# Value rows moved to partitions 32 to 95, mean rows placed by GpSimd and ScalarE copies, gate columns made by halves of the bank

## The chip, the core and the metric

The kernel runs on one core of one Trainium2 chip. The metric is the device time of one execution in microseconds (us); a kernel's figure is the median of several executions, 483.07 us before the change.

## The reference, cut to what matters

Two stages follow each other: a windowed attention with block summaries, and an expert layer that picks 384 tokens for each expert in turn.

```python
B, H, S, D = 4, 8, 768, 64
k_sum = k.reshape(B, H, 24, 32, D).max(axis=3)      # one key per block of 32
v_sum = v.reshape(B, H, 24, 32, D).mean(axis=3)     # one value per block of 32
scores_l = where(|i - j| < 16, q @ k.T / 8, -1e9)
scores_s = q @ k_sum.T / 8 + log(32)
a = softmax(concat(scores_l, scores_s))
x = a @ concat(v, v_sum)                            # then laid out as 3072 tokens x 512
logits = x @ w_gate                                 # 8 experts
# (token, expert) pairs in falling order of logit, at most 384 tokens an expert, one expert a token
out[tokens of e] = relu(x[tokens of e] @ w1[e]) @ w2[e]
```

## The kernel before

**Tiles.** A batch has 12 query blocks of 64 tokens. Two blocks and all heads of one sort make a unit `u`; two units (even and odd heads) make a tile `t`, so there are 24 tiles, six for each of the 4 batches. For a query block the kernel holds 120 key columns: 64 + 2 x 16 tokens of the window (`W` = 96) and 24 block summaries (`C` = 120). The values stand in a tile `VW` (two buffers, for even and odd batches) of 120 partitions x 12 blocks x 8 heads x 73 columns: in one row the 64 value columns, 8 gate columns (value times gate weights) and a 1 for the sum of the softmax.

**Steps of a tile.** `s` (PE, L407) makes the scores; `m` (DVE, L415) adds the mask and takes the row maximum; `e` (ACT, L422) takes the exponential; `t` (PE, L138) transposes; `c` (ACT or DVE, L183/L185) copies the transpose to `pt`; `pv` (PE, L447) multiplies with `VW`; `n` (DVE, L467 to L472) divides; `xw` (POOL's queue, L499) writes the token rows `xd` to memory.

**Steps of a batch, before its tiles.** `k`, `q`, `vt`, `w` are loads issued by SyncE (SP). `w` (L348) brings the value rows of two query blocks each into partitions 0 to 63 of `VW`, six times a batch; L350 brings the last 32 rows into partitions 64 to 95. `vh` (POOL, L297) and `vs` (DVE, L303) sum the values of a block of 32. `vg` (PE, L312) multiplies the values with the gate weights; its results for the even blocks stand in rows 0 to 63 of the bank `VL` and for the odd blocks in rows 64 to 127. `vgc` (L185 or L183) copies them as gate columns into `VW`. `h` (POOL or ACT) copies the first 32 rows of the next block into partitions 64 to 95, the part of the window that reaches into it. `vm` (PE) transposes the mean rows, `vmc` (L328 or L330) copies them into partitions 96 to 119 of block 0, and `place` puts the same 24 rows beside the other 11 blocks: for batch 0 by eleven copies of ACT and POOL, for batches 1 to 3 by one DMA of SP (L340) from partitions 96 to 119 of block 0 to the same partitions of blocks 1 to 11.

**What sets the order.** Every step is a task with an engine, a cost, its predecessors and a rank. `plan` keeps a clock for each engine from these costs and writes the tasks out one by one, by start and rank; `TUNE` and `RANK` hold the numbers. So the order on each engine is fixed when the program is built, and an instruction that waits holds all that stands behind it on its engine. SP's loads share a ring in which each issue waits for the DMA eight places ahead of it.

**After attention** the routing of expert 0 and eight experts follow (PE lines L929, L940, L963, L908).

Of the kernel before, what the change touches and what calls it, by code (L numbers as in the profile page):

```python
# [19 lines left out]
B, H, S, D = 4, 8, 768, 64  # L20
# [3 lines left out]
NB = S // BLK  # L24
# [32 lines left out]
def attention_moe(ctx, tc, qT, kT, vT, v73, wg, w1r, w2r, cst, out, dbg=None, dbi=None):  # L57
# [131 lines left out]
    with ExitStack() as att:  # L189
# [64 lines left out]
        for b in range(B):  # L254
# [32 lines left out]
            for p in range(HP):  # L287
# [5 lines left out]
                @task(("vh", b, p), "pool", 0.9, [("vt", b, p)] + ([("vs", b, p - 1)] if p else []), u0 + TUNE["vs"] + 0.1 * p)  # L293
# [5 lines left out]
                @task(("vs", b, p), "dve", 0.5, [("vh", b, p)], u0 + TUNE["vs"] + 0.1 * p)  # L299
# [5 lines left out]
                @task(("vg", b, p), "pe", 0.9, [("vt", b, p)] + ([("vg", b, p - 1)] if p else [("m", u0 - 6 + k) for k in range(2)] + [("vmc", b - 1, 1)] + [("vgc", b - 1, int(b == 1), x) for x in range(2)] if b else ["constants"]), u0 + TUNE["vg"] + 0.1 * p)  # L305
# [46 lines left out]
            for j, (k0, k1) in enumerate(((0, 2), (2, NQ // 2)) if b == 0 else ((0, NQ // 2),)):  # L352
                for x in range(2):
                    @task(("vgc", b, j, x), {"act": 0.42 + 0.06 * (k1 - k0), "dve": 0.3 + 0.07 * (k1 - k0)}, None, [("vg", b, HP - 1)] + [("w", b, k) for k in range(k0, k1)], u0 + TUNE["vc"] + 0.1 * x + j)
                    def _(eng, b=b, x=x, k0=k0, k1=k1):
                        vw = VW[b % 2]
                        for s in range(2):
                            copy(eng, vw[:QB, 2 * k0 + x:2 * k1:2, s::2, s * D:s * D + E], VL[b][x * QB:x * QB + QB, k0:k1, s::2])
                        if x == 0 and k1 == NQ // 2:
                            copy(eng, gates(vw[QB:W, NQ - 1]), VL[b][QB - 2 * HALO:QB, k1].rearrange("p (k s) e -> p k s e", s=2))  # L360

                for k in range(k0, k1):
                    @task(("h", b, k), "pool" if b else {"pool": 1.2 if k else 0.65, "act": 1.0 if k else 0.55}, 1.2 if k else 0.65, [("vgc", b, j, x) for x in range(2)] + ([("vgc", b, 0, x) for x in range(2)]), u0 + TUNE["hv"] + 0.1 * k)
                    def _(eng=None, b=b, k=k):
                        i = max(2 * k - 1, 0)
                        copy(eng or nc.gpsimd, VW[b % 2][QB:W, i:2 * k + 1], VW[b % 2][:2 * HALO, i + 1:2 * k + 2])
# [23 lines left out]
        for u in range(U):  # L390
# [40 lines left out]
            def _(eng, u=u):  # L431
# [4 lines left out]
                  [("c", u), ("c", u | 1 if t < NT - 1 else u), ("w", b, i // 2)] + ([("place", b)] if b else [("place", b, i - s + x) for x in range(2) if i - s + x]) + [("h", b, k) for k in (i // 2, i // 2 + 1) if k < NQ // 2]  # L436
# [14 lines left out]
        for t in range(NT):  # L451
# [22 lines left out]
            if t + 1 in ends:  # L474
                @task(("lr", t), "dve", 0.53 if t < NT - 3 else 0.27, [("n", t)], u + TUNE["n"] + (2.5 if t < NT - 4 else 0.0))
# [21 lines left out]
            @task(("xw", t), "pool", 0.6, [("xm" if t == NT - 1 else "n", t)], u, 0.8)  # L497
# [543 lines left out]
```

## Time and profile before

| | us |
|---|---|
| median of 3 runs | 483.07 (481.05 to 485.16) |
| the profiled execution | 481.45 |
| its span, first to last instruction | 479.6 |
| last `pv` of attention starts | 149.54 |
| last write of token rows issued by POOL | 154.80 |

The span is the profiled execution without 1.85 us that lie around it. The first 155 us are attention, the rest is routing and experts. Engines are PE (matmul), PEld (its weight load), DVE, ACT, POOL and SP; "idle before, releaser" names what ended an engine's wait, and "issue" is a wait for nothing that the profile shows. Partitions are the 128 rows of the on-chip memory.

### The profile page before, as it was taken

The numbers are of one execution on the slowest core, as the hardware profiler recorded it, in microseconds if no ns is written. First come the engines' busy times: TensorE is split into PE (matmuls) and PEld (weight loads), VectorE is DVE, ScalarE is ACT, GpSimd is POOL, SyncE is SP. The second block draws the span as 40 slices with busy tenths as digits, with TensorE's granted clock in tenths as the row PEclk, the third lists the DMA queues.
The fourth block names the chain that finished last, engine by engine and source line by source line (L and its number), as shares of the span: only waits on it lengthen the run. The fifth ranks groups of instructions, "written<-read, shape, count | busy, mean of one in ns | idle before, by whom it ended". The sixth has DMA issues, their size and how long they took to land.

```text
span 479.6 us, 11577 instructions
## 1 busy us (share of the span) xinstructions
PE 433.3 (90%) x4381; PEld 377.4 (79%) x4381; DVE 341.4 (71%) x1285; ACT 219.6 (46%) x469; POOL 128.2 (27%) x190
## 2 busy tenths in 40 slices
PE   7667949959795489999999999999999999999995
PEld 7557739759684379878978978978988988988985
DVE  5367774956887688888879878978978877662520
ACT  5586664953794035426306414424424524652420
POOL 3375552642611120023023024004003203501001
PEclk9669886976898569999999999999999999999998
DMA  8999999997422064085067058039129118950101
GB/s 302 236 402 226 355 201 247 359 224 204 103 84 94 27 236 191 0 275 216 1 230 262 1 187 282 24 126 326 41 93 322 77 44 299 388 186 22 45 22 44
DMA packets 25555, 84.02 MB, mean 175 GB/s; under 512 B 3461, under 2 KB 3845, under 8 KB 25117
## 3 DMA queue, kind: packets, MB, share of 16 engines
q1 hardware_dynamic: 19740, 62.84, 42.3%
q0 software_dynamic: 5760, 20.45, 11.7%
q8 instruction: 34, 0.56, 0.5%
q14 instruction: 21, 0.16, 0.1%
HBM read 68.06 MB, written 13.37 MB: 170 GB/s over the span
## 4 chain that ended last, share of the span: by engine, by line
PE 81%; issue 6%; DMA 6%; DVE 5%; SPq 1%; ACT 0%; POOLq 0%; DVEq 0%; POOL 0%
PE h L940 28%; PE y L963 25%; PE o L447 6%; PE t L138 5%; PE l L312 3%; PE s L407 3%; DMA vw<-v 3%; PE r L533 2%; PE y L908 2%; PE h L138 2%; PE x L407 2%; DMA vt<-vT 2%; DMA xg<-xd,idx 1%; DVE xq L472 1%; PE h L929 1%
## 5 line engine op out<-in xcount | busy, mean ns | idle before, releaser
L735 POOL DMA_INDIRECT xg<-xd,idx x24 | 24.9, 1037 | 165.5 <-issue 119.3
L963 PE MATMUL y<-bh,hl 128*128 128x512 f32 x168 | 67.6, 402 | 0.0
L963 PE MATMUL y<-bl,hh 128*128 128x512 f32 x168 | 67.2, 400 | 0.0
L963 PE MATMUL y<-bh,hh 128*128 128x512 f32 x168 | 66.6, 397 | 0.0
L720 ACT ACTIVATE ah<-raw 128x1024 fp32r<-128x1024 f32 (+1 forms) x36 | 34.3, 970 | 65.2 <-DMA raw<-w1r 37.7
L945 ACT ACTIVATE hh<-h 128x384 fp32r<-128x384 f32 x64 | 31.5, 492 | 68.5 <-PE h L940 66.9
L422 ACT ACTIVATE pe<-sm,mx 128x120 f32<-128x120 f32 x192 | 58.2, 385 | 4.1 <-DVE mx L415 4.0
L940 PE MATMUL h<-xh,al 128*128 128x384 f32 x256 | 55.7, 339 | 0.0
L940 PE MATMUL h<-xl,ah 128*128 128x384 f32 x256 | 55.0, 339 | 0.0
L940 PE MATMUL h<-xh,ah 128*128 128x384 f32 x244 | 54.7, 342 | 0.0
L890 POOL DMA_INDIRECT out<-y,idx x24 | 29.2, 1216 | 86.2 <-ACT y L888 63.4
L948 DVE SCALAR_TENSOR_TENSOR hl<-h,hh 128x384 fp32r<-128x384 f32 x64 | 34.7, 549 | 24.4 <-ACT hh L945 23.9
L940 PEld LDWEIGHTS h<-xh,al 128*128 128x128 f32 x256 | 45.3, 188 | 0.0
L940 PEld LDWEIGHTS h<-xl,ah 128*128 128x128 f32 x256 | 45.1, 188 | 0.0
L940 PEld LDWEIGHTS h<-xh,ah 128*128 128x128 f32 x244 | 42.9, 188 | 0.6
L183 ACT ACTIVATE pt<-t 120x512 f32<-120x512 f32 x44 | 25.2, 591 | 36.7 <-PE t L138 36.5
L447 PE MATMUL o<-vw,pt 120*64 120x73 f32 x736 | 34.9, 253 | 7.1 <-issue 5.0
L447 PEld LDWEIGHTS o<-vw,pt 120*64 120x64 f32 x736 | 30.8, 156 | 11.2 <-issue 7.5
L723 DVE TENSOR_TENSOR bl<-raw,bh 128x1024 fp32r<-128x1024 f32 x32 | 38.9, 1217 | 0.8 <-ACT bh L720 0.8
L723 DVE TENSOR_TENSOR al<-raw,ah 128x1024 fp32r<-128x1024 f32 (+1 forms) x36 | 39.1, 1100 | 0.1
L963 PEld LDWEIGHTS y<-bh,hh 128*128 128x128 f32 x168 | 31.6, 188 | 5.6
L963 PEld LDWEIGHTS y<-bl,hh 128*128 128x128 f32 x168 | 31.6, 188 | 5.5
(183 smaller groups left out, 809.2 us busy)
## 6 DMA issues: line engine op xcount, KB each, us to landing
raw<-w1r SPq DMA_DIRECT2D x32, 512.0 KB, 5.5
raw<-w2r SPq DMA_DIRECT2D x32, 512.0 KB, 4.5
vw<-v SPq DMA_DIRECT2D x24, 292.0 KB, 19.0
xd<-xq POOLq DMA_DIRECT2D x24, 288.0 KB, 6.8
kd<-kT SPq DMA_DIRECT2D x16, 400.0 KB, 9.7
vt<-vT SPq DMA_DIRECT2D x16, 400.0 KB, 8.6
qt<-qT SPq DMA_DIRECT2D x3, 1536.0 KB
vw<-vw SPq DMA_DIRECT2D x3, 602.2 KB
```

What stands on the lines that cost most here:

```text
L138: nc.tensor.transpose(o, i, idn)
L183: nc.scalar.activation(o, i, AF.Copy)
L422: nc.scalar.activation(PE_[u][:, p], SM[u][0][:, p], AF.Exp, bias=SM[u][1][:, p:p + 1], scale=-1.0)
L447: nc.tensor.matmul(po(t, s)[x * 64:x * 64 + 64, p], PT[u][:, p, x * 64:x * 64 + 64], VW[b % 2][:C, i - s + x, 2 * p + s], start=True, stop ...
L720: nc.scalar.activation(hi[:, c], raw[:, c], AF.Copy)
L723: nc.vector.tensor_tensor(lo[:, c], raw[:, c], hi[:, c].bitcast(F32), op=OP.subtract)
L735: nc.gpsimd.indirect_dma_start(out=x, out_offset=None, in_=xd, in_offset=bass.IndirectOffsetOnAxis(ap=idx[:, c:c + 1], axis=0))
L890: st = nc.gpsimd.indirect_dma_start(out=out, out_offset=bass.IndirectOffsetOnAxis(ap=ROUND[r][1][:, c:c + 1], axis=0), in_=y, in_offset=None)
L940: nc.tensor.matmul(ph, a[:, d], b[:, d], start=k == d == 0, stop=k == 2 and d == 3, skip_group_check=r == 0 and f in early)
L945: nc.scalar.activation(hh[:, f], ph, AF.Relu)
L948: nc.vector.scalar_tensor_tensor(hl[:, f], ph, 0.0, hh[:, f].bitcast(F32), op0=OP.max, op1=OP.subtract)
L963: nc.tensor.matmul(py[c], a[:, f, s], b, start=f == 0 and i == 0, stop=f == 7 and i == 2)
```

## The change

The value rows of a block now stand in the order halo, block, means: rows 0 to 31 of `VW` are the first 32 tokens of the window, rows 32 to 95 the other 64. The six loads of a batch go into partitions 32 to 95; one load brings rows 0 to 31 of block 0; `h` copies partitions 64 to 95 of a block into partitions 0 to 31 of the next. In the bank `VL` the first six blocks have rows 0 to 63, the last six rows 64 to 127, and `vgc` has four copies (first or last six blocks, lower or upper 32 rows), each waiting for three of the six loads. The DMA of `place` is gone; all four batches have eleven `place` copies on POOL or ACT. A `pv` of a tile needs the `place` copies of its own two blocks and one `h`. All numbers of `RANK` and five of `TUNE` are replaced, so every engine's order is another.

```diff
-    sm=4, spe=0, sdve=0.11, sact=0, spool=1.08, m=0.569, e=2.793, t=2.307, c=0.793,
+    sm=4, spe=0.03, sdve=0.14, sact=0.59, spool=1.01, m=0.569, e=2.793, t=2.307, c=0.793,
...
                     for i in range(NQ + 1):
-                        c, x = min(i * QB, SP - QB), i % 2 * QB
-                        o = VL[b][x:x + QB, i // 2, 2 * p:2 * p + 2].rearrange("p h e -> p (h e)")
+                        k, x = (i // 2, i % 2) if i < NQ else (NQ // 2, 0)
+                        c = QB * (NQ // 2 * x + k) + 2 * HALO if i < NQ else 0
+                        o = VL[b][x * QB:x * QB + QB, k, 2 * p:2 * p + 2].rearrange("p h e -> p (h e)")
...
-            for i in range(1, NQ) if b == 0 else ():
-                @task(("place", b, i), {"pool": 0.63, "act": 0.6}, None, [("vmc", b, 0), ("vmc", b, 1)], TUNE["p0"] + 0.5 * i)
-                def _(eng, i=i):
-                    copy(eng, VW[0][W:C, i], VW[0][W:C, 0])
-
-            @task(("place", b), "sp", 0.6, [("vmc", b, 0), ("vmc", b, 1)] + ([("pv", u0 - NQ - 1)] if b > 1 else []), u0 + TUNE["pl"], 1.7) if b else lambda f: None
-            def _(b=b):
-                vw = VW[b % 2]
-                nc.sync.dma_start(vw[W:C, 1:].rearrange("p n h d -> p n (h d)"), vw[W:C, :1].rearrange("p n h d -> p n (h d)").to_broadcast([NB, NQ - 1, H * VD]))
+            for i in range(1, NQ):
+                @task(("place", b, i), {"pool": 0.67, "act": 0.67}, None, [("vmc", b, 0), ("vmc", b, 1)] + ([("pv", u0 - 2 * NQ + i // 2 * 2 + 1)] if b > 1 else []), u0 + TUNE["pl"] + 0.5 * i)
+                def _(eng, b=b, i=i):
+                    copy(eng, VW[b % 2][W:C, i], VW[b % 2][W:C, 0])
...
-                    nc.sync.dma_start(vw[:QB, 2 * k:2 * k + 2], bass.AP(tensor=v.tensor, offset=v.offset + 2 * k * QB * H * VD, ap=[[H * VD, QB], [QB * H * VD, 2], [1, H * VD]]))
-                    if k == NQ // 2 - 1:
-                        nc.sync.dma_start(vw[QB:W, NQ - 1], v[S:])
+                    if k == 0:
+                        nc.sync.dma_start(vw[:2 * HALO, 0], v[:2 * HALO])
+                    nc.sync.dma_start(vw[2 * HALO:W, 2 * k:2 * k + 2], bass.AP(tensor=v.tensor, offset=v.offset + (2 * k * QB + 2 * HALO) * H * VD, ap=[[H * VD, QB], [QB * H * VD, 2], [1, H * VD]]))
...
+            for x in range(2):
+                for y in range(2):
+                    @task(("vgc", b, x, y), {"act": 0.55 + (0.22 if x == y == 0 else 0.0), "dve": 0.55 + (0.22 if x == y == 0 else 0.0)}, None, [("vg", b, HP - 1)] + [("w", b, k) for k in range(3 * x, 3 * x + 3)], u0 + TUNE["vc"] + x + 0.1 * y)
...
+                        copy(eng, dst, VL[b][x * QB + 32 * y:x * QB + 32 * y + 32, :6].rearrange("p n (k s) e -> p (n k) s e", s=2))
...
+                    i = max(2 * k, 1)
+                    copy(eng or nc.gpsimd, VW[b % 2][:2 * HALO, i:2 * k + 2], VW[b % 2][QB:W, i - 1:2 * k + 1])
```

On SP, from the loads of batch 1's mean rows on, this stands before (`vw_102` is the value tile of batches 1 and 3, `vw_101` of batches 0 and 2; `24x11x584` is `place`):

```order
L291 DMA vt<-vT 128x800 x3
L340 DMA vw_102<-vw_102 24x11x584
L260 DMA qt_99<-qT 128x3072
L348 DMA vw_101<-v 64x2x584 x6
L350 DMA vw_101<-v 32x584
```

and this now:

```order
L291 DMA vt<-vT 128x800 x3
L260 DMA qt_99<-qT 128x3072
L345 DMA vw_101<-v 32x584
L346 DMA vw_101<-v 64x2x584 x6
L291 DMA vt<-vT 128x800 x4
```

The DMA that waited for DVE's copy of the mean rows is gone from between the loads, and the queries and values of batch 2 follow batch 2's `vt` directly.

On POOL, around the tiles of batch 1, before (`32x584` and `32x1168` are `h`, `vh` the block sums of batch 2, `kd` the window and summary columns of batch 2's keys):

```order
L185 COPY vw_102<-vw_102 32x584
L185 COPY vw_102<-vw_102 32x1168 x5
L185 COPY kd<-kd 128x12x36
L185 COPY kd<-ks 128x12x24
L185 COPY kd<-kd 128x12x36 x2
L297 TENSOR_TENSOR vh<-vt 128x384
```

and now:

```order
L297 TENSOR_TENSOR vh<-vt 128x384
L185 COPY vw_102<-vw_102 24x584 x3
L297 TENSOR_TENSOR vh<-vt 128x384
L497 DMA xd<-xq_103 128x576
L185 COPY vw_102<-vw_102 24x584
L185 COPY kd<-kd 128x12x36
L185 COPY kd<-ks 128x12x24
L185 COPY vw_102<-vw_102 24x584
L185 COPY kd<-kd 128x12x36
```

Ten copies of `24x584` for batch 1 are new on POOL, and they stand between the `vh` and `kd` work of batch 2 and the writes of token rows.

On DVE, at the start of batch 0, before:

```order
L303 TENSOR_REDUCE vs<-vh 128x24
L185 COPY pt<-t 120x512
L185 COPY vw_101<-l 64x4x4x8 x2
L303 TENSOR_REDUCE vs<-vh 128x24
L273 TENSOR_REDUCE ks<-kd 128x24 x2
```

and now:

```order
L185 COPY pt<-t 120x512 x2
L303 TENSOR_REDUCE vs<-vh 128x24
L185 COPY vw_101<-l 32x24x2x8 x3
L331 TENSOR_SCALAR vw_101<-x 24x4x2x64
```

The last `vs` of batch 0 stood behind the gate copies that wait for the value loads and now stands ahead of them; the copy of the mean rows follows on the same engine.

## Rows read from the trace of the kernel before

**Rows 1.** Stages of attention: length, busy us of each engine, granted clock, DMA.
```profile
core 0: us, PE busy (x) PEld busy (x) DVE busy (x) ACT busy (x) POOL busy (x), PEclk, DMA share, GB/s
12.00:58.00 46.00, 35.83 (x658) 30.56 (x654) 28.25 (x138) 30.77 (x84) 23.85 (x37) 0.78 1.03 304
58.00:73.00 15.00, 8.17 (x188) 7.27 (x188) 10.41 (x72) 8.99 (x28) 8.84 (x13) 0.82 1.03 217
...
94.00:105.00 11.00, 6.00 (x133) 5.01 (x132) 7.92 (x53) 7.86 (x24) 7.50 (x12) 0.85 1.03 196
...
sum 143.00, PE 113.10 PEld 97.17 DVE 99.41 ACT 92.27 POOL 64.37; mean PE 16.16 PEld 13.88 DVE 14.20 ACT 13.18 POOL 9.20
```
**Rows 2.** DMA view: GB/s in 40 slices of 1 us, 0 to 40 us.
```profile
GB/s 0 48 285 384 346 211 346 385 374 412 422 406 400 290 173 206 203 208 206 206 213 223 216 296 368 399 406 407 386 391 404 402 406 408 399 454 436 366 198 175
```
**Rows 3.** The same, 120 to 160 us.
```profile
GB/s 0 135 128 128 139 105 5 0 0 251 309 60 272 9 0 16 0 221 74 0 101 210 0 124 179 0 0 281 14 76 221 290 18 0 0 46 249 0 8 0
```
**Rows 4.** The page's DMA issues: count, KB each, us to landing; and the instruction queue.
```profile
q8 instruction: 34, 0.56, 0.5%
...
vw<-v SPq DMA_DIRECT2D x24, 292.0 KB, 19.0
xd<-xq POOLq DMA_DIRECT2D x24, 288.0 KB, 6.8
...
vw<-vw SPq DMA_DIRECT2D x3, 602.2 KB
```
**Rows 5.** Timeline, start of batch 0: start, duration, work, idle before and releaser.
```profile
25.48 0.69 ACT L183 ACTIVATE vw<-l 64x128 f32<-64x128 f32 x3 [2.91 <-DMA vw<-v]
26.20 0.50 DVE L185 COPY vw<-l 64x128 f32<-64x128 f32 x2 [4.42 <-ACT vw L183]
26.62 0.54 DVE L303 TENSOR_REDUCE vs<-vh 128x24 f32<-128x384 f32 x1
...
29.06 0.59 ACT L328 ACTIVATE vw<-x 24x512 f32<-24x512 f32 x1
```
**Rows 6.** Chain of waits: start, length, what.
```profile
12.19 13.27 DMA vw<-v
...
31.81 1.97 PE o L447 x32
...
43.11 2.48 issue
...
125.58 2.50 issue
```
**Rows 7.** Timeline of PE around the first tiles of batches 1 and 2.
```profile
58.26 1.24 PE L447 MATMUL o<-vw,pt 120*64 120x73 f32 x32
...
71.82 1.36 PE L312 MATMUL l<-wgp,vt 128*64 128x16 f32 x22 [5.44 <-issue]
...
73.09 2.10 PE L447 MATMUL o<-vw,pt 120*64 120x73 f32 x30
...
78.55 2.21 PE L447 MATMUL o<-vw,pt 120*64 120x73 f32 x32
...
94.30 1.24 PE L447 MATMUL o<-vw,pt 120*64 120x73 f32 x32
...
104.65 0.83 PE L312 MATMUL l<-wgp,vt 128*64 128x16 f32 x13 [4.69 <-issue]
105.32 2.19 PE L447 MATMUL o<-vw,pt 120*64 120x73 f32 x32
```
**Rows 8.** Stages after the two stops: length, PE busy, granted clock, DMA.
```profile
76.00:82.00 6.00, 6.00 (x84) 0.57 1.03 252
82.00:94.00 12.00, 11.60 (x231) 1.00 1.02 387
...
105.00:118.00 13.00, 13.00 (x210) 0.60 0.89 252
```
**Rows 9.** Waits: who for whom, us in total, times, longest.
```profile
SPq L340 <- DVE dn L468: 17.1, 2, 11.0
```
**Rows 10.** Timeline: the `place` copies of batch 0 on ACT and POOL.
```profile
29.98 3.58 ACT L183 ACTIVATE vw<-vw 24x584 f32<-24x584 f32 x6
...
30.02 3.15 POOL L185 COPY vw<-vw 24x584 f32<-24x584 f32 x5 [0.25 <-ACT vw L328]
```
**Rows 11.** Groups by line, 0 to 175 us: busy us, mean ns.
```profile
L183 ACT ACTIVATE vw<-l 64x192 f32<-64x192 f32 (+3 forms) x18 | 4.2, 276 | 7.1 <-PE l L312 4.0 <-DMA vw<-v 2.9
...
L185 DVE COPY vw<-l 64x192 f32<-64x192 f32 (+1 forms) x6 | 1.8, 334 | 5.5 <-ACT vw L183 5.5
```
**Rows 12.** Waits of POOL, 24 to 130 us.
```profile
POOL vh L297 <- DVE vs L303: 25.9, 9, 7.4
```

More of the change, by code (lines that the diff above doesn't have):

```diff
@@ L291, in _ @@
                     nc.sync.dma_start(vt[p], vT[b, p])
-                @task(("vh", b, p), "pool", 0.9, [("vt", b, p)] + ([("vs", b, p - 1)] if p else []), u0 + TUNE["vs"] + 0.1 * p)
+                @task(("vh", b, p), "pool", 1.0, [("vt", b, p)] + ([("vs", b, p - 1)] if p else []), u0 + TUNE["vs"] + 0.1 * p)
                 def _(b=b, p=p):
@@ L303, in _ @@
                     nc.vector.tensor_reduce(VS[b][:, p], VH[b, p], axis=AX.X, op=OP.add)
-                @task(("vg", b, p), "pe", 0.9, [("vt", b, p)] + ([("vg", b, p - 1)] if p else [("m", u0 - 6 + k) for k in range(2)] + [("vmc", b - 1, 1)] + [("vgc", b - 1, int(b == 1), x) for x in range(2)] if b else ["constants"]), u0 + TUNE["vg"] + 0.1 * p)
+                @task(("vg", b, p), "pe", 0.9, [("vt", b, p)] + ([("vg", b, p - 1)] if p else [("m", u0 - 6 + k) for k in range(2)] + [("vmc", b - 1, 1)] + [("vgc", b - 1, x, y) for x in range(2) for y in range(2)] if b else ["constants"]), u0 + TUNE["vg"] + 0.1 * p)
                 def _(b=b, p=p):
@@ L347, in _ @@
                     vw, v = VW[b % 2], v73[b]
-                    nc.sync.dma_start(vw[:QB, 2 * k:2 * k + 2], bass.AP(tensor=v.tensor, offset=v.offset + 2 * k * QB * H * VD, ap=[[H * VD, QB], [QB * H * VD, 2], [1, H * VD]]))
-                    if k == NQ // 2 - 1:
-                        nc.sync.dma_start(vw[QB:W, NQ - 1], v[S:])
[L352 to L366, printed above, removed]
@@ new lines, in _ @@
+                    if k == 0:
[4 more added lines that the diff above has]
+                    @task(("vgc", b, x, y), {"act": 0.55 + (0.22 if x == y == 0 else 0.0), "dve": 0.55 + (0.22 if x == y == 0 else 0.0)}, None, [("vg", b, HP - 1)] + [("w", b, k) for k in range(3 * x, 3 * x + 3)], u0 + TUNE["vc"] + x + 0.1 * y)
+                    def _(eng, b=b, x=x, y=y):
+                        vw, r = VW[b % 2], 2 * HALO * (1 + y)
+                        dst = vw[r:r + 32, 6 * x:6 * x + 6].rearrange("p n h d -> p (n h) d")
+                        (hs, _), cols = dst.ap[-2:]
+                        dst = bass.AP(tensor=dst.tensor, offset=dst.offset, ap=[list(dst.ap[0]), [2 * hs, 6 * HP], [hs + D, 2], [1, E]])
+                        copy(eng, dst, VL[b][x * QB + 32 * y:x * QB + 32 * y + 32, :6].rearrange("p n (k s) e -> p (n k) s e", s=2))
+                        if x == y == 0:
+                            copy(eng, gates(vw[:2 * HALO, 0]), VL[b][:2 * HALO, 6].rearrange("p (k s) e -> p k s e", s=2))
@@ L368, in keys, with _ @@
+            for k in range(NQ // 2):
+                @task(("h", b, k), "pool" if b else {"pool": 1.16 if k else 0.65, "act": 1.17 if k else 0.66}, 1.16 if k else 0.65, [("vgc", b, x, y) for x in range(2 if k > 2 else 1) for y in range(2)], u0 + TUNE["hv"] + 0.1 * k)
+                def _(eng=None, b=b, k=k):
+                    i = max(2 * k, 1)
+                    copy(eng or nc.gpsimd, VW[b % 2][:2 * HALO, i:2 * k + 2], VW[b % 2][QB:W, i - 1:2 * k + 1])
         def keys(b, p, r, i):
@@ L384, in before_s @@
             b = t // 6 if t == 3 else (t + 3) // 6
-            return [("vmc", b, x) for x in range(2)] + [("vgc", b, int(b == 0), x) for x in range(2)] if t == 3 or t > 6 and t % 6 == 1 else []
+            return [("vmc", b, x) for x in range(2)] + [("vgc", b, x, y) for x in range(2) for y in range(2)] if t == 3 or t > 6 and t % 6 == 1 else []
         def bank(t):
@@ L435, in _ @@
             @task(("pv", u), "pe", TUNE["cp"],
-                  [("c", u), ("c", u | 1 if t < NT - 1 else u), ("w", b, i // 2)] + ([("place", b)] if b else [("place", b, i - s + x) for x in range(2) if i - s + x]) + [("h", b, k) for k in (i // 2, i // 2 + 1) if k < NQ // 2]
+                  [("c", u), ("c", u | 1 if t < NT - 1 else u), ("w", b, i // 2)] + [("place", b, i - s + x) for x in range(2) if i - s + x] + [("h", b, i // 2)]
                   + ([("m", 2), ("m", 3)] if t == 0 else [("n", t - 2 if t == NT - 1 else t - 1)] if t != NT - 2 else [("vmc", B - 1, x) for x in range(2)]) + ([("pv", u - 1)] if s else []), u)
@@ L474, in attention_moe @@
             if t + 1 in ends:
-                @task(("lr", t), "dve", 0.53 if t < NT - 3 else 0.27, [("n", t)], u + TUNE["n"] + (2.5 if t < NT - 4 else 0.0))
+                @task(("lr", t), "dve", 0.8 if t < NT - 3 else 0.27, [("n", t)], u + TUNE["n"] + (2.5 if t < NT - 4 else 0.0))
                 def _(t=t):
@@ L495, in _ @@
                         nc.scalar.activation(XS[:, 2 * k + s, c], po(t, s)[:, k, c], AF.Copy, scale=DN[t][:, 1, h:h + 1])
-            @task(("xw", t), "pool", 0.6, [("xm" if t == NT - 1 else "n", t)], u, 0.8)
+            @task(("xw", t), "pool", 0.55, [("xm" if t == NT - 1 else "n", t)], u, 0.8)
             def _(t=t, XS=XS):
```

6 lines of the change are left out of this document (3 added, 3 removed).

## The prediction

> **What bounds the kernel now.** I read the stages first. The experts behind 155 us keep their instructions; I cost them at nothing and look at attention only. From 12 to 155 us PE is busy for 113.1 us, DVE for 99.4, ACT for 92.3 and POOL for 64.4 of 143 [rows 1]: no engine is full on average. But the DMA share is 1.03 in the stages from 12 to 105 us, while the rate swings between 196 and 321 GB/s [rows 1]. The DMA engines are always occupied and often slow.
>
> The view of the DMAs by microsecond says when. Loads into all 128 partitions run at about 400 GB/s (386 to 408 between 25 and 34 us); while the six value loads of batch 0 go into partitions 0 to 63, nine slices in a row stand at 173 to 223, 206 in the middle [rows 2]. Short packets are not the reason: the token rows, 288 KB in pieces like the values', reach 251 and 309 GB/s in neighbouring slices [rows 3]. `place`, 602.2 KB into 24 partitions [rows 4], runs alone at 128 to 139 GB/s for 4.5 us [rows 3].
>
> The chain of waits shows who suffers: it runs over the value loads from 12.19 to 25.46 us, and the first `pv` starts at 31.81 [rows 6]. After that the tiles of one batch follow each other every 3.1 us at best (five steps from 78.55 to 94.30), but the step into batch 1 takes 14.8 us (58.26 to 73.09) and that into batch 2 11.0 (94.30 to 105.32) [rows 7]. In both PE stands for 5.44 and 4.69 us inside a series of equal multiplications, waiting for nothing that the profile shows [rows 7]; two such stops of 2.5 us stand at 43.11 and 125.58 [rows 6]. My reading, not shown: PE waits for its own instructions, which the page has as a queue on the same 16 DMA engines [rows 4]. [...]
>
> **The change, part by part.** All is summed against the profiled execution, 481.45 us, 1.6 below the median of the runs.
>
> *Value loads.* A batch's six loads and the short one are 6 x 292 + 73 KB = 1.83 MB, 8.9 us at 206 GB/s. No row shows 64 partitions that begin at 32. The bounds are 206 (same width, other place) and 405 GB/s (all rows). `place` moves 130/24 = 5.4 GB/s per partition, the values 206/64 = 3.2; so a partition can take more than the values give it, and 64 x 5.4 = 344 GB/s is my value, 5.3 us. That is 3.6 us less a batch, 0 to 4.4 at the bounds. The trace shows that partitions 0 to 63 are halved against 128. [...]
>
> *Start.* Today the landing at 25.46 releases the gate copies, DVE's last `vs` stands behind them at 26.62, the mean rows come at 29.06 [rows 5], the first `pv` at 31.81. The loads land 3.6 us earlier. `vs` now stands ahead of the gate copies, so the mean rows no longer wait for the loads either; from the landing to the first `pv` are 6.35 us today, of which the stretch up to 29.06 is 3.6. I take 2.4 of it. Together -6.0 (bounds: 0 and -9).
>
> *Batch boundaries.* Over the best step of 3.1 the two long ones lose 11.7 + 7.9 = 19.6 us. `place` is 4.5 us of transfer and stands behind loads; SP's queue was held at it for 17.1 us in two waits [rows 9], and queries and values of the next batch stood behind it. Both go, and the first tile of a batch needs one `place` copy where it needed the whole DMA. The stops inside PE should shorten with less on the DMA engines: 1.8 MB of `place` gone and four slow loads shortened, 3 x 4.5 + 4 x 3.6 = 28 us of DMA time against the 93 that are full. Late next are the block sums and gate copies, so not all comes back: -12.0 (0 to -19.6).
>
> *Clock.* At full clock the 19 us at 0.57 and 0.60 would be 6 x 0.57 + 13 x 0.60 = 11.2, so 7.8 are lost. Some stops stay: -3.0 (0 to -7.8).
>
> *The two small stops:* -2.0 of 5 (0 to -5.0).
>
> *New copies.* Batches 1 to 3 get 33 `place` copies, by the order 32 on POOL and one on ACT; five took 3.15 us on POOL, 0.63 each, and six 3.58 on ACT [rows 10]. With two more `h` copies on POOL in place of ACT, about 1.1 each by their neighbours in size, POOL gets 20.2 + 2.2 = 22.4 us. Its 64.4 become 87 of some 127 us. It has room, but works in order: the copies stand between `vh`, which waited 25.9 us for DVE's `vs` [rows 12], and the writes of token rows. Hidden altogether it costs 0, in the path altogether 22.4; I take +6.5, because a batch's POOL work (64.4/4 + 7.5 = some 24 us) is close to six tile steps of 3.1 plus the batch's gate products.
>
> *Gate copies.* 24 copies cost 4.2 + 1.8 = 6.0 us [rows 11]. Now 16 of 384 elements: at 512 elements ACT took 0.59 [rows 5], so 0.45 each and 8 us with the four short ones: 2 us more on two engines, +0.5 (0 to 2).
>
> SP saves three issues; the shifted loads have room on its queue. `RANK` moves everything else; I cost that at nothing, because the tasks and the planner stay, and it is the least certain line.
>
> Sum: -6.0 - 12.0 - 3.0 - 2.0 + 6.5 + 0.5 = -16.0. That gives 465.45 for the profiled execution and **467.0** against the median.
>
> **The rivals.**
>
> *POOL becomes the bound.* For: POOL 7.5 of 11 us busy in the second boundary [rows 1] with no `place` on it. Against: 79 idle us in the 143. If two thirds of the 22.4 lie in the path (15 for 6.5), the gain falls to 7.5: 475.6.
>
> *The value loads stay at 206 GB/s.* Then only `place` and the order count: start -2.4, boundaries -8, clock -1.5, stops 0, copies and gates +5: -6.9, 476.2. For it: nothing in the trace shows 64 partitions above 223 GB/s. [...] Against: the 5.4 GB/s per partition of `place`.
>
> *Slower: POOL's queue holds the first tile of each batch.* The place is the `24x584` copies of a batch behind `vh` of the next, on POOL. If those `vh` wait for their loads and for `vs` as they did [rows 12], `pv` of the new batch waits for POOL, and boundaries and clock give nothing back: -6.0 - 2.0 + 22.4 + 0.5 = +14.9, 498. It decides from the point where more than 7.5 of the 22.4 us lie in the path and the long steps remain.
>
> *The change doesn't relieve PE.* If the stops have nothing to do with the DMA load and the new order loses what `place` gave, start and copies cancel: 483.
>
> **How the numbers follow.** A change below 1%, 4.8 us, can't be told from none. Forecast case 0.66, of it 0.06 below 455, POOL as the bound 0.11, loads at 206 GB/s 0.10, no relief 0.07, slower 0.06. The predicted time is that of the first case. If all gains came whole, 41 us, DVE and ACT would have to be busy for 97% and 90% of the stretch; in the best one, 82 to 94 us, PE was at 97% [rows 8], but that held for 12 us. I allow 28 us of gain, 455. Upward the range takes in both weaker gains and a little more: 479. It leaves out 0.06 below and 0.13 above. Faster by over 1% (below 478.2): the first three cases less 0.02 at their upper edge, 0.85. Within 1%: 0.09. Slower: 0.06.
>
> **What would show it.** DMA slices of the value loads near 344 to 400 GB/s instead of 206, and a DMA share below 1 before 105 us; a first `pv` near 26 us; steps into batches 1 and 2 of 5 to 8 us; "issue" stops inside a PE series under 3 us; a granted clock above 0.8 behind them; POOL near 87 us busy, its `24x584` copies not named as releaser of PE; last `pv` near 133 us and all later stages as long as now. Value loads at 206, or `pv` waiting for POOL's copies, would make it wrong, as would a stretch behind attention that changes by more than 2 us.

## The result, and the profile after

The changed kernel takes 454.38 us (median of 4 runs, 453.77 to 455.45) against 483.56 us for the kernel before in the same job: a ratio of 0.940 [0.936, 0.945], 29 us less. The forecast was 467.0 (455 to 479). The direction was right and the gain nearly twice as large. The profiled execution took 454.78 us, its span 453.0; 26.7 us less than the profiled execution before.

Stages of attention after, columns as in [rows 1]:

```profile
core 0: us, PE busy (x) PEld busy (x) DVE busy (x) ACT busy (x) POOL busy (x), PEclk, DMA share, GB/s
12.00:58.00 46.00, 39.75 (x860) 33.85 (x858) 40.64 (x223) 38.83 (x108) 35.02 (x49) 0.95 1.03 392
58.00:73.00 15.00, 14.38 (x290) 12.36 (x290) 12.12 (x58) 11.86 (x33) 12.07 (x21) 0.92 0.98 364
73.00:94.00 21.00, 20.12 (x457) 17.24 (x454) 19.97 (x106) 18.14 (x53) 19.16 (x29) 1.00 0.45 164
94.00:105.00 11.00, 10.02 (x232) 8.40 (x230) 10.63 (x65) 10.48 (x32) 10.85 (x15) 1.00 0.27 102
...
sum 116.00, PE 100.03 PEld 85.06 DVE 103.74 ACT 94.20 POOL 87.75; mean PE 20.01 PEld 17.01 DVE 20.75 ACT 18.84 POOL 17.55
```

The granted clock is at 0.92 to 1.00 where it was 0.78 to 0.85 [rows 1], and from 73 us on the DMA engines are less than half occupied. The sum is over 12 to 128 us. POOL is busy for 19.16 of 21 us in the third stage.

The rate in 40 slices of 1 us from 0 to 40 us, as in [rows 2], and the page's row for the value loads, as in [rows 4]:

```profile
GB/s 0 57 139 329 405 416 409 382 400 413 410 381 392 290 394 386 416 380 396 388 406 406 405 395 384 413 410 394 396 462 440 406 419 265 350 362 402 403 405 412
...
vw<-v SPq DMA_DIRECT2D x24, 292.0 KB, 10.0
```

From 14 us on, where nine slices stood near 206 GB/s, they stand at 380 to 416; a value load lands after 10.0 us instead of 19.0.

PE around the first `pv` tiles (L445) of batches 0, 1 and 2, as in [rows 7]:

```profile
23.94 1.24 PE L445 MATMUL o<-vw,pt 120*64 120x73 f32 x32
...
48.01 1.17 PE L445 MATMUL o<-vw,pt 120*64 120x73 f32 x29
...
56.09 2.51 PE L313 MATMUL l<-wgp,vt 128*64 128x16 f32 x55 [0.93 <-issue]
58.33 0.38 PE L445 MATMUL o<-vw,pt 120*64 120x73 f32 x1
...
77.13 1.24 PE L445 MATMUL o<-vw,pt 120*64 120x73 f32 x32
...
84.72 0.28 PE L445 MATMUL o<-vw,pt 120*64 120x73 f32 x1
...
102.70 1.24 PE L445 MATMUL o<-vw,pt 120*64 120x73 f32 x32
105.64 1.24 PE L445 MATMUL o<-vw,pt 120*64 120x73 f32 x32
```

Set against the starts of the same tiles before ([rows 7]; batch 1's first tile started at 72.92, just ahead of the row at 73.09, batch 2's last tile at 133.57, batch 3's first at 136.50), this gives where the time came from:

| stretch of `pv` starts | before | after | difference |
|---|---|---|---|
| to the first tile | 31.7 | 23.9 | -7.8 |
| inside batch 0 | 26.5 | 24.1 | -2.4 |
| step into batch 1 | 14.7 | 10.3 | -4.3 |
| inside batch 1 | 21.4 | 18.8 | -2.6 |
| step into batch 2 | 11.0 | 7.6 | -3.4 |
| inside batch 2 | 28.3 | 18.0 | -10.3 |
| step into batch 3 | 2.9 | 2.9 | 0.0 |
| inside batch 3 | 13.0 | 15.0 | +1.9 |

Together -28.9 up to the last `pv`, which starts at 120.60; from there to the end of the span it is 332.4 us instead of 330.1, so 2.3 are given back. The largest single piece is inside batch 2. PE's stops for nothing that the profile shows came to 18.8 us from 12 us to the last `pv`; now it is 3.3.

The chain of waits (start, length, what) shows what batch 3 lost:

```profile
105.48 0.27 issue
105.75 2.54 POOL vw L185 x4
108.29 0.49 POOL xd L497
108.79 1.99 POOL vw L185 x3
110.82 1.24 PE o L445 x32
```

Seven `place` copies of the last batch stand in front of its second tile; that step takes 5.2 us.

### The profile page after: what moved, and what is told of

It is laid out like the page before. It is cut to its first block, busy times and chain, and to the rows that moved or that the text cites. A ratio compares the mean times of both kernels' runs of the same rounds, so it can differ in the third digit from the quotient of the medians.

```text
span 453.0 us, 11636 instructions
## 1 busy us (share of the span) xinstructions
PE 421.0 (93%) x4387; PEld 365.4 (81%) x4387; DVE 344.2 (76%) x1286; ACT 219.7 (49%) x463; POOL 150.4 (33%) x224
## 4 chain that ended last, share of the span: by engine, by line
PE 81%; DVE 6%; DMA 5%; issue 4%; ACT 2%; POOL 1%; POOLq 0%; SPq 0%; DVEq 0%; ACTq 0%
PE h L938 30%; PE y L961 26%; PE t L138 4%; PE o L445 4%; PE l L313 3%; PE r L531 3%; PE y L906 2%; PE h L138 2%; PE s L405 2%; DMA vt<-vT 2%; DMA xg<-xd,idx 1%; DVE xq L470 1%; POOL vw L185 1%; DMA kd<-kT 1%; DVE sm L413 1%
## 5 line engine op out<-in xcount | busy, mean ns | idle before, releaser
L733 POOL DMA_INDIRECT xg<-xd,idx x24 | 23.8, 993 | 167.7 <-issue 119.7
L185 POOL COPY vw<-vw 24x584 f32<-24x584 f32 (+2 forms) x60 | 48.0, 828 | 4.3 <-issue 3.1
L445 PE MATMUL o<-vw,pt 120*64 120x73 f32 x736 | 30.8, 234 | 6.3 <-DVE xq L470 2.2
L961 PEld LDWEIGHTS y<-bh,hl 128*128 128x128 f32 x168 | 31.7, 189 | 5.3
```

What stands on the lines that cost most here:

```text
L185: eng.tensor_copy(o, i)
L445: nc.tensor.matmul(po(t, s)[x * 64:x * 64 + 64, p], PT[u][:, p, x * 64:x * 64 + 64], VW[b % 2][:C, i - s + x, 2 * p + s], start=True, stop ...
L733: nc.gpsimd.indirect_dma_start(out=x, out_offset=None, in_=xd, in_offset=bass.IndirectOffsetOnAxis(ap=idx[:, c:c + 1], axis=0))
L961: nc.tensor.matmul(py[c], a[:, f, s], b, start=f == 0 and i == 0, stop=f == 7 and i == 2)
```

## The experiments

**The three parts apart.** The change has three separable parts: the layout (rows 32 to 95, with the gate copies by halves that go with it), the copies of `place`, and the numbers (`TUNE`, `RANK`). The layout also brings other costs for the planner to count with (`vh` 1.0 for 0.9, `vs` 0.55 for 0.5, `lr` 0.8 for 0.53, `xw` 0.55 for 0.6), so its order differs too. Six kernels give the other combinations.

The kernel before with the new numbers alone:

```diff
-RANK = {('w', 0): -14.83, 'place': 5.98, 'c': -18.99, ...
+RANK = {'k': 1.26, ('vs', 0): -21.07, ('vt', 0): 7.56, ...   (and five numbers of TUNE)
```

> The kernel before with the TUNE and RANK of the change, its layout, loads and place DMA as before. If the gain is relief of the DMA engines (theory A), the new order alone gives little: 478 to 488 us. If the part of the gain that the prediction missed, some 13 us, lies in the order (theory B), it shows here: 465 to 473.

The kernel before with the copies alone:

```diff
-            for i in range(1, NQ) if b == 0 else ():
+            for i in range(1, NQ):
                 @task(("place", b, i), ...
-            @task(("place", b), "sp", ...
```

> The kernel before with place by POOL and ACT copies in all batches, its layout, loads and numbers otherwise as before. Theory A: 13 us of DMA time and SP's wait at place go, 470 to 477 us. If the copies on POOL cost what the prediction took (6.5 us) or more and the loads at 206 GB/s stay the bound: 480 to 488.

With the copies and the numbers, on the old layout (both edits above):

> Layout and loads as before (partitions 0 to 63), place by copies, numbers of the change. Copies alone gave 0 and numbers alone 4 us: 478 to 481 without interplay. If the numbers need the copies but not the faster loads: 468 to 473.

The changed kernel with `place` of batches 1 to 3 by DMA again and the old numbers, so the layout alone (the second edit above undone):

> Value rows in partitions 32 to 95, h and gate copies of the change, but place for batches 1 to 3 by one DMA and the numbers of the kernel before. Theory A: the loads run near 400 GB/s, the first pv starts some 4 to 6 us earlier, 14 to 18 us of DMA time go; 470 to 476 us, the stop inside PE ahead of batch 1 shorter than 5.4 us. If the rate of the loads is hidden: 481 or more.

The same with the new numbers:

> Layout and numbers of the change, place of batches 1 to 3 by one DMA. The layout alone gave some 19 us and the numbers alone 4, so without interplay 460 to 462. If the numbers' worth comes from the POOL copies that they were made for, 460 to 465; if it comes from the loads at twice the rate, 452 to 457, and the copies are worth nothing.

The changed kernel with the old numbers:

> The changed kernel with the TUNE and RANK of the kernel before. Theory A: most of the gain stays, 455 to 462 us, with value loads near 400 GB/s. Theory B: the order carries the missing 13 us, so 465 to 470.

| layout | `place` | numbers | us | ratio | first `pv` | last `pv` | stops of PE up to it, us |
|---|---|---|---|---|---|---|---|
| old | DMA | old | 483.56 | 1 | 31.7 | 149.5 | 18.8 |
| old | DMA | new | 479.92 | 0.994 [0.990, 0.997] | 30.1 | 145.4 | 9.7 |
| old | copies | old | 483.32 | 0.999 [0.995, 1.003] | 30.8 | 150.7 | 12.7 |
| old | copies | new | 468.73 | 0.969 [0.963, 0.975] | 29.2 | 134.8 | 4.2 |
| new | DMA | old | 464.71 | 0.967 [0.955, 0.979] | 31.1 | 128.7 | 6.7 |
| new | DMA | new | 464.54 | 0.963 [0.956, 0.969] | 23.4 | 128.5 | 5.5 |
| new | copies | old | 469.21 | 0.976 [0.964, 0.987] | 31.7 | 133.2 | 3.8 |
| new | copies | new | 454.38 | 0.940 [0.936, 0.945] | 23.9 | 120.6 | 3.3 |

Worked out from the medians, and from the ratios where these differ by more than 1 us, three things follow. The layout is worth 11 to 19 us in all four pairs. The copies are worth nothing on the old kernel, seem to cost 4 us on the new layout with the old numbers (the two intervals overlap), and bring 10 to 12 with the new ones, on either layout. The numbers are worth 0 to 2 us (new layout; not clear of noise) or 3 to 4 (old) with the DMA, and 14 to 17 with the copies. So 11 to 15 of the 29 us belong neither to the copies nor to the numbers but to the pair. These first-`pv` times are of one execution each; profiles of kernels that agree in all of batch 0 scatter from 23.2 to 25.7 with the new numbers, and from 29.3 to 31.7 with the old.

*The start* needs both the layout and the numbers: 23.4 and 23.9 against 29.2 to 31.7 in the six others. POOL's timeline (start, duration, work, idle before and releaser) says why the layout alone doesn't do it. With the layout alone:

```profile
16.14 1.00 POOL L297 TENSOR_TENSOR vh<-vt 128x384 f32<-128x384 f32 x1 [0.67 <-DVE vs L303]
21.66 1.76 POOL L185 COPY vw<-vw 32x584 f32<-32x584 f32 x2 [4.52 <-ACT vw L183]
23.82 1.15 POOL L185 COPY vw<-vw 32x1168 f32<-32x1168 f32 x1 [0.39 <-ACT vw L183]
25.05 1.00 POOL L297 TENSOR_TENSOR vh<-vt 128x384 f32<-128x384 f32 x1
```

After:

```profile
14.55 1.01 POOL L297 TENSOR_TENSOR vh<-vt 128x384 f32<-128x384 f32 x1 [1.08 <-DVE vs L303]
17.70 1.01 POOL L297 TENSOR_TENSOR vh<-vt 128x384 f32<-128x384 f32 x1 [2.14 <-DVE vs L303]
20.14 6.17 POOL L185 COPY vw<-vw 32x584 f32<-32x584 f32 x8 [1.43 <-issue]
```

In the first, the batch's last `vh` stands behind `h` copies that wait 4.52 us for ACT's gate copies, so the block sums, the mean rows and the first tile wait for the value loads however early those land. In the second it stands ahead of all of them and starts 7.35 us earlier.

*The copies with the old numbers.* The groups of `place` copies by engine, 12 to 128 us, with the old numbers (count | busy us, mean ns):

```profile
L183 ACT ACTIVATE vw<-vw 24x584 f32<-24x584 f32 x28 | 17.4, 677 | 0.4
L185 POOL COPY vw<-vw 24x584 f32<-24x584 f32 x16 | 10.1, 672 | 0.2
```

and in the changed kernel:

```profile
L185 POOL COPY vw<-vw 24x584 f32<-24x584 f32 x37 | 24.2, 680 | 0.8
L183 ACT ACTIVATE vw<-vw 24x584 f32<-24x584 f32 x7 | 4.3, 675 | 0.1
```

A copy costs the same on both engines. The old numbers give 28 of 44 to ACT. ACT there, in batch 2:

```profile
100.80 1.27 ACT L183 ACTIVATE vw<-vw 24x584 f32<-24x584 f32 x2
102.09 0.60 ACT L183 ACTIVATE pt<-t 120x512 f32<-120x512 f32 x1
102.71 1.27 ACT L183 ACTIVATE vw<-vw 24x584 f32<-24x584 f32 x2
104.00 0.60 ACT L183 ACTIVATE pt<-t 120x512 f32<-120x512 f32 x1
104.62 2.42 ACT L183 ACTIVATE vw<-vw 24x584 f32<-24x584 f32 x4
107.06 4.68 ACT L420 ACTIVATE pe<-sm,mx 128x120 f32<-128x120 f32 x16
```

and PE behind it:

```profile
107.50 2.47 PE L138 MATMUL t<-cs,pe 128*120 128x128 f32 x8 [1.79 <-ACT pe L420]
```

Eight copies for batch 3 stand ahead of the exponentials of batch 2's tiles, and PE's transposes wait for those. That kernel is 8 us ahead of the layout alone at batch 2's first tile (84.0 against 92.3) and 5 behind at batch 3's (120.9 against 115.9).

**The engine of the copies, with the order kept.** In the old-numbers kernel every copy of batches 1 to 3 goes to POOL at its place in the program (ACT 8, POOL 36):

```diff
-                    copy(eng, VW[b % 2][W:C, i], VW[b % 2][W:C, 0])
+                    copy(nc.gpsimd if b else eng, VW[b % 2][W:C, i], VW[b % 2][W:C, 0])
```

> The changed kernel with the old numbers (469.2 us; 28 of the 44 copies of the mean rows on ACT, 16 on POOL), where every copy of batches 1 to 3 that stood on ACT is given to POOL at the same place in the program, so that ACT has 8 and POOL 36, about as in the changed kernel (7 and 37). The order of all other instructions is kept. If the 14.8 us that the new numbers bring with the copies are the copies' engine (ACT's copies stand ahead of its exponentials, and PE waits for those), 455 to 461 us. If they are the order of the rest (the first pv at 31.7 us against 23.9 alone is 7.7 us), this stays at 465 to 472 us. The first pv should stay near 31.7 us in both cases, since batch 0 is not touched; so the best for the first theory is some 461.

In the changed kernel 24 of the 33 copies go to ACT (ACT 30, POOL 14):

```diff
-                    copy(eng, VW[b % 2][W:C, i], VW[b % 2][W:C, 0])
+                    copy(nc.scalar if b and i % 3 else eng, VW[b % 2][W:C, i], VW[b % 2][W:C, 0])
```

> The changed kernel with 24 of the 33 copies of the mean rows of batches 1 to 3 given to ACT at the same place in the program (ACT 30, POOL 14 instead of 7 and 37); the order of all other instructions is kept. If the copies' engine decides, ACT's 14.6 us of added work lie in the path ahead of the exponentials as with the old numbers: 463 to 469 us, with PE waiting for ACT's exponentials. If the order of the rest decides, 453 to 458 us.

Measured: 475.46 us, 0.986 [0.980, 0.992], and 464.45 us, 0.963 [0.957, 0.969]. So the first is 5 to 6 us slower than with its copies on ACT, which neither theory said (the intervals overlap; the last `pv` starts at 138.5 instead of 133.2), and the second is 10 us slower than the changed kernel, as the engine's theory said. One place of the first, on PE at the second tile of batch 1:

```profile
63.66 2.22 PE L445 MATMUL o<-vw,pt 120*64 120x73 f32 x32 [2.35 <-POOL kd L185]
```

and the largest wait of PE's in the second, from 24 to 126 us (who for whom: us in total, times, longest):

```profile
PE t L138 <- ACT pt L183: 6.0, 5, 2.4
```

On the old order PE now waits for what stands in POOL's queue; on the new one it waits for ACT's copies of the transposed tiles, with ACT busy for 107.2 of 116 us; the expected wait for the exponentials is not among PE's large ones. Neither the engine nor the order of the rest is the cause by itself: the numbers chose the two together.

**The DMA back in, with the order kept.** The 33 copies become one DMA a batch, issued where the first copy stood:

```diff
-                    copy(eng, VW[b % 2][W:C, i], VW[b % 2][W:C, 0])
+                    vw = VW[b % 2]
+                    if b == 0:
+                        copy(eng, vw[W:C, i], vw[W:C, 0])
+                    elif i == 1:
+                        nc.sync.dma_start(vw[W:C, 1:]..., vw[W:C, :1]....to_broadcast([NB, NQ - 1, H * VD]))
```

> The changed kernel with the 33 copies of the mean rows of batches 1 to 3 replaced by one DMA a batch, issued where the first copy stood; every other instruction keeps its place on its engine. If the gain of the copies with their own numbers is the order of the other instructions, and not that the DMA is gone, this stays within 3 us of the changed kernel: 452 to 458 us. If the DMA itself costs (4.5 us of transfer, SP held at it until the mean rows are there, the tiles behind both), this comes near the version with rows 32 to 95 and the DMA in its own order: 462 to 468 us.

Measured: 463.95 us, 0.963 [0.960, 0.967], as the DMA's theory said: 10 us worse than the copies, with every other instruction in its place. PE there:

```profile
58.76 0.48 PE L449 MATMUL o<-vw,pt 120*64 120x73 f32 x2
62.89 2.18 PE L449 MATMUL o<-vw,pt 120*64 120x73 f32 x30 [3.65 <-DMA vw<-vw]
68.06 1.24 PE L449 MATMUL o<-vw,pt 120*64 120x73 f32 x32
```

The first tile of batch 1 stands for 3.65 us behind the DMA, after two of its 32 multiplications. The step from the first to the second tile takes 9.3 us in batch 1 and 9.2 in batch 2, where the changed kernel has 4.3 and 4.2: these two steps are the 10 us.

For the last batch alone:

```diff
-                    if b == 0:
+                    if b < B - 1:
```

> The changed kernel with the eleven copies of the last batch alone replaced by one DMA; there no loads stand behind it on SP, and POOL's copies stood in the chain of waits for 4.5 us in that batch. If they cost what the chain says, 451 to 453 us. If the chain only swaps them for the DMA's own 4.5 us, 454 us; if the DMA's wait for its transfer is longer than the first copies, up to 457 us.

Measured: 453.65 us, 0.942 [0.938, 0.945], which can't be told from the changed kernel's 0.940. The last batch's steps sum to 13.4 us instead of 15.0, so 1.6 of the 1.9 lost there do come from POOL's copies, but too little reaches the end for a faster version to be claimed.

**What POOL's copies cost now.** Without the 22 copies of batches 2 and 3 (their mean rows are left out, but for block 0):

```diff
-                    copy(eng, VW[b % 2][W:C, i], VW[b % 2][W:C, 0])
+                    if b < 2:
+                        copy(eng, VW[b % 2][W:C, i], VW[b % 2][W:C, 0])
```

> The changed kernel without the place copies of batches 2 and 3 (their blocks 1 to 11 keep the mean rows of batches 0 and 1): 22 copies, some 14 us less on POOL. If POOL's copies cost 6.5 of 22.4 us as predicted: 4 us less, 450 us. If they are hidden: 453 to 455. If POOL has become the bound of the second half: 445 to 448.

And with every copy of batches 1 to 3 made twice:

```diff
+                    for _ in range(2 if b else 1):
+                        copy(eng, VW[b % 2][W:C, i], VW[b % 2][W:C, 0])
```

> The changed kernel with each place copy of batches 1 to 3 done twice, 33 copies and some 21 us more, nearly all on POOL. Share in the path of 0.3 as predicted: 460 to 462 us. Hidden: under 457. POOL the bound: 468 to 475.

Measured: 452.49 us, 0.936 [0.931, 0.941], and 468.02 us, 0.968 [0.963, 0.973]. Taking some 14 us of copies off saves 1.9 by the medians, with intervals that overlap the changed kernel's; adding some 21 costs 13.6, at the edge of what was expected of POOL as the bound. POOL's room held one set of copies and does not hold a second.

**The stops of PE.** The kernel before, without the value loads of batches 2 and 3:

```diff
+                    if b > 1:
+                        return
                     nc.sync.dma_start(vw[:QB, 2 * k:2 * k + 2], ...
```

> The kernel before without the value loads of batches 2 and 3 (it leaves these values out and multiplies what batches 0 and 1 left there). It takes about 18 us of slow transfer away between 60 and 115 us and moves no other instruction. If PE's stops of 5.44 and 4.69 us are its waits behind DMAs that are slow because they fill partitions 0 to 63, the stops in the steps into batches 1 and 2 go below 1.5 us and the time falls by 8 to 12 us. If the stops come from something else (the place DMA, the order of the instructions), they stay at 4 us or more, the steps into batches 1 and 2 stay at 14.8 and 11.0 us and the time falls by less than 4 us.

Measured: 477.97 us, 0.991 [0.987, 0.994]; between the two expectations and nearer to the second. Its stops:

```profile
70.32 1.36 PE L312 MATMUL l<-wgp,vt 128*64 128x16 f32 x22 [4.90 <-issue]
100.42 0.83 PE L312 MATMUL l<-wgp,vt 128*64 128x16 f32 x13 [2.41 <-issue]
123.53 1.73 PE L449 MATMUL o<-vw,pt 120*64 120x73 f32 x24 [2.87 <-issue]
```

The same two series still stop, for 4.90 and 2.41 us instead of 5.44 and 4.69, and batch 2 still takes 27.9 us inside. The DMA share within these three stops (windows, columns as in [rows 1]):

```profile
65.40:70.30 4.90, 0.02 (x1) 0.00 (x0) 2.29 (x11) 1.29 (x5) 2.78 (x5) 0.84 0.95 311
98.00:100.40 2.40, 0.01 (x1) 0.00 (x0) 2.30 (x18) 1.99 (x7) 1.79 (x4) 0.79 0.81 319
120.60:123.50 2.90, 0.07 (x3) 0.00 (x0) 2.87 (x20) 2.15 (x7) 2.90 (x4) 0.97 0.15 28
```

The third stands at a share of 0.15, the stop of 2.50 us before [rows 6] at 0.09: within these two hardly a DMA engine is at work. That does not clear the DMA engines. The trace also holds the packets of the instruction queue, q8 in [rows 4], of 16,384 bytes each. In the kernel before, count all that PE runs (multiplications, weight loads, its sequencer's own): between its six stops of over 1 us lie 768, 512, 256, 1024 and 768 instructions, always a multiple of 256, and every 256 have one such packet.

| stop of PE, before | its packet starts | has landed | PE goes on | after the landing |
|---|---|---|---|---|
| 14.58, 2.17 us | 13.84 | 15.31 | 16.75 | 1.44 |
| 43.11, 2.48 us | 42.58 | 43.92 | 45.59 | 1.67 |
| 60.09, 1.27 us | 58.70 | 59.84 | 61.35 | 1.51 |
| 66.38, 5.44 us | 68.95 | 70.31 | 71.82 | 1.51 |
| 99.97, 4.69 us | 101.74 | 103.05 | 104.65 | 1.60 |
| 125.58, 2.50 us | 125.78 | 126.70 | 128.09 | 1.38 |

Of the 53 stops of over 0.7 us from 12 us to the last `pv` in the profiles of all twenty kernels, 45 stand at such a place, and each of these ends 1.2 to 1.7 us after its packet has landed; the other eight are not explained. So what PE stands for are its instructions, as the prediction had read it. Their packet comes late because it starts late: before, from 16 to 120 us, it starts 1.5 to 8.4 us (5.3 in the middle) after PE has begun the 256 instructions ahead of it; at 128 and 136 us, with the DMA engines idle, 1.1 us after and 0.4 us ahead. The stop at 125.58 has its cause ahead of it: its packet waited 6.0 us, for most of which `place` went at 128 to 139 GB/s [rows 3], and started at 125.78, as `place` ended. The third stop above is the same: `place` until 121, the packet at 121.09. Without the value loads the packet of batch 2's stop waits 6.7 us instead of 8.4.

Then the other direction: 24 added loads (to a buffer that nobody reads) in the changed kernel from 83 us on, where its DMA engines are less than half busy, into all 128 partitions, into 0 to 63, and into 32 to 95:

```diff
+                for j in range(24 if t == 12 else 0):
+                    more = sb.tile([128, SP], F32, name="vt", bufs=HP)
+                    nc.sync.dma_start(more[:128], kT[j % B, j % HP, :128])
```

> The changed kernel with 24 added loads of 400 KB over 128 partitions into spare buffers, issued from about 85 us on, where the DMA engines are 17 to 40% busy; nothing reads them. If PE's stops inside a series are its instructions waiting behind data on the DMA engines: stops of 2 to 5 us appear between 85 and 115 us and the time rises by 3 to 10 us, 457 to 464. If they are not: 453 to 456 and stops under 1.2 us as before.

> The same with the 24 loads into partitions 0 to 63 only, half the bytes. If what holds PE's instructions is data that goes slowly into half of the partitions: as long as or longer than the run before, 457 to 466, with stops of 2 to 5 us. If only the bytes count, half of it.

> The changed kernel plus the same 24 added loads of 64 partitions as before (196.6 KB each), now into partitions 32 to 95. SP needed 26.93 us to issue the 24 loads into 0 to 63 and 34.80 us for twice the bytes into all 128 partitions; SP's ring holds eight, so this time is that of the transfers. If the place of the 64 partitions sets the rate, 32 to 95 has the rate of all 128: half the bytes of the wide loads, so near 17 us. If only the number of partitions counts, 27 us as for 0 to 63. The kernel's time says little here: 454 to 456 us either way.

Measured: 455.43 us, 0.942 [0.937, 0.948]; 455.12 us, 0.941 [0.936, 0.947]; 455.56 us, 0.947 [0.942, 0.951]. The windows of the wide one:

```profile
84.00:96.00 12.00, 11.11 (x225) 9.10 (x222) 11.66 (x44) 9.91 (x29) 11.47 (x21) 1.00 0.99 335
96.00:108.00 12.00, 11.76 (x270) 10.18 (x273) 11.73 (x80) 11.43 (x36) 11.96 (x17) 1.00 0.98 341
```

A share of 0.99 with PE busy for 11.1 and 11.8 of 12 us, at full clock, no stop above 0.6 us. The added loads do hold PE's packets up: from 85 to 119 us these start 2.1 to 5.0 us after PE has begun the 256 instructions ahead, where the changed kernel has 0.3 to 1.6. But PE needs 5.0 to 7.4 us for 256 instructions there, a packet some 1 us and PE 1.3 to 1.6 more, so only the wait of 5.0 us was too long: that is the stop of 0.57 us at 93.33. Full DMA engines alone neither stop PE for long nor lower its clock here. Of the rate these runs say nothing: SP took 34.80 us for the wide 24, 26.93 for the low, 25.62 for those into 32 to 95, where 17 were expected. 4.7 MB in 25.62 us are 184 GB/s, less than [rows 2] show for partitions 0 to 63, so something else than the partitions set that pace.

**The rate, by split loads.** Each value load of the changed kernel as two, by partitions (32 to 63, 64 to 95):

```diff
+                    for y in range(2):
+                        r = 2 * HALO * (1 + y)
+                        nc.sync.dma_start(vw[r:r + 32, 2 * k:2 * k + 2], ...
```

> The changed kernel, its order kept, each value load split into two DMAs of 32 partitions (32 to 63, 64 to 95). If what doubles the rate is that one load reaches partitions on both sides of 64, the value loads fall back to about 206 GB/s and the time rises by what the rate is worth: theory A 462 to 468 us. If only the number of partitions or the order counts: 454 to 456.

or, as a control with as many DMAs, by query block:

```diff
+                    for y in range(2):
+                        nc.sync.dma_start(vw[2 * HALO:W, 2 * k + y], ...
```

> The control to the run before: the same twelve DMAs of 146 KB a batch, split by query block, each over partitions 32 to 95. Theory A: loads near 380 to 400 GB/s, 454 to 457 us. If the count of DMAs is what costs in the run before, this one is as long as it.

Measured: 464.60 us, 0.964 [0.958, 0.970], and 460.33 us, 0.951 [0.946, 0.957]. The control itself loses 6 us, so the number of DMAs costs more than what was to be told apart. The landings tell the rates: where batch 1's loads follow each other, those split by block land 0.37 us apart (404 GB/s), those split by partitions 0.49 to 0.55 (some 290). With the layout alone, whole loads land 0.73 to 0.74 us apart, twice 0.37; before, 1.27 to 1.40. So 64 partitions from 32 on keep the rate in halves of the size, 32 partitions do not, and the 4.3 us between the two runs go with that. The control's 6 us go with SP: one issue takes 0.5 to 0.6 us there, longer than the transfer, and from 14 to 18 us the DMA share falls to 0.62 from 1.05.

## Why the prediction missed

**The step that failed** is "`RANK` moves everything else; I cost that at nothing". With the old numbers, layout and copies give 469.21 us, 12 to 14 less than before (by ratio and by median), somewhat under the -16.0 of the sum. That nearness is luck: there the start gave nothing instead of -6.0 (31.7 in both), while the three steps between batches gave 18.3 us. The new numbers are worth another 15 to 17 on top, and that term was missing. In the changed kernel 15.3 us were gained inside batches 0 to 2, where the sum had little but the clock and the two small stops, -5.0. The line on `RANK` was called the least certain, yet neither the range nor a rival had it: the limit of 28 us of gain came from the busy shares, and 29 were had.

**Value loads.** 344 GB/s was taken from `place`; the slices show 380 to 416, nearer to the upper bound of 405. The rival of 206 GB/s is out: with the layout alone, too, the value loads land after 9.3 us.

**Start, -6.0.** It came to -7.8 in the profiled execution (-6.0 to -8.5 over those that agree in batch 0), but not by the loads alone. With the new layout and the old numbers the loads land early and the first `pv` stays at 31.1 and 31.7. That the order has its share was right (`vs` ahead of the gate copies, not tested apart); POOL's `h` ahead of `vh`, which the prediction didn't look at, stood in the same way.

**Boundaries, -12.0.** The two steps gave 4.3 + 3.4 = 7.7 back, to 10.3 and 7.6 us where 5 to 8 were expected. That `place` by DMA costs 5 us in each of batches 1 and 2 is shown, but on the new order; on the old kernel nothing was gained without it: there the step from the first to the second tile grew to 11.2 and 9.5 us, with stops of PE for its instructions of 2.92 and 3.21 us.

**Clock and stops, -3.0 and -2.0.** Too small: the stops fell by 15.5 us (18.8 to 3.3), part of which the sum has in its boundaries, and the clock came back, to 0.92 to 1.00 in the four stages shown. The reading behind it, that PE waits for its own instructions, which come late behind transfers, is borne out by the packets: 45 of 53 stops end 1.2 to 1.7 us after one has landed, and `place` held one up until it was over. Not shown is how much of the delay goes to `place` and how much to the loads into partitions 0 to 63. The order has its part as well: the new numbers alone halve the stops (18.8 to 9.7) on the old loads. The 19 us of the -3.0 are the 6 at 0.57 and the 13 at 0.60 of [rows 8]; that they would have been 7.8 us shorter at full clock was the author's estimate, and no run shows it apart.

**What the layout's 11 to 19 us are** is not settled. The stops of PE account for 0.9 to 12.1 us of it in the four pairs. Taking half of the slow loads away altogether gave the kernel before 3.8 to 4.6 us, so transfer time by itself is likely the smaller part; the halved gate copies and the other order that the plan makes from them and from the changed costs were not run without the faster loads.

**New copies, +6.5.** Mis-sized: 22 of the 33 cost 1.9 us by the medians, not clear of noise, and the steps of batch 3 show the place. POOL is busy for 87.75 us to 128, as worked out, and its copies do release PE, for 1.1 us in all. On the new layout with the old numbers the same copies cost some 4.5 us as planned and 10.8 with POOL for nearly all; the 6.5 lies between the two.

**Gate copies, +0.5,** were not measured apart. The stretch behind the last `pv` grew by 2.3 us, slightly past the limit of 2 that the prediction set itself; over the twenty kernels, which differ in attention only, it is 330.1 to 334.6 us, so the 2.3 can't be put down to the change.

## What to carry to other kernels

Where a plan fixes each engine's order, a new table of numbers is a term of its own: list which engine each moved step lands on and what stands behind it there, and give the term a range as wide as the idle time it could close, because parts of a change can be worth nothing apart and 10 to 15 us together. An engine's idle sum tells whether work fits, its queue tells whether it is hidden: POOL and ACT need the same time for a `place` copy (672 to 680 ns), and the choice was worth 10 us here on the order made for it. Where PE stops for nothing that the profile shows, count its instructions up to the stop and look when the packet of the next ones started; the DMA load that held it up can stand ahead of the stop, as here for the one of 2.50 us at 125.58, with a DMA share of 0.09 inside it.

## What was not expected of the hardware

Value loads into 64 partitions that begin at 32 run at 380 to 416 GB/s, as loads into all 128 do (386 to 408 [rows 2]), where those into 0 to 63 take 206; the added loads into 32 to 95, of another form, ran at 184, and why is open. Splitting the 24 value loads into 48 cost 6 to 10 us (460.33 and 464.60 against 454.38) though the bytes stayed the same. The instruction queue brought packets of 16,384 bytes, one for every 256 instructions that PE ran (before: 17 packets up to the last `pv`, and 17 such places). In the kernel before, at a DMA share of 1.03 [rows 1], one packet started 8.4 us after PE had begun the 256 ahead of it, and PE then stood for 4.69 us; another started 7.6 us after, and PE stood for 5.44. A stop outlasted the transfer that held its packet up: the one of 2.50 us at 125.58, at a DMA share of 0.09.
